# Attention inside a feed-forward kernel: working on whole pairs of heads at a time

## The chip, the cores and the metric

The kernel runs on one core of one Trainium2 chip. A core has five instruction queues that run beside each other and meet through semaphores: TensorE (PE in the profile; its weight loads are listed apart as PEld), VectorE (DVE), ScalarE (ACT), GpSimd (POOL) and SyncE (SP), which here only issues DMAs. Each queue works strictly in the order in which its instructions were written. The metric is the device time of one launch in microseconds (us), as the median of several runs.

## The reference

Two things are computed one after the other. First comes causal attention with a window of 128 positions and a slope per head, for 8 batches of 8 heads, 576 positions and 64 channels:

```
scores = q @ k.T / sqrt(64) + bias(head, distance)      # kept where 0 <= distance < 128
attn   = exp(scores - max) / (sum + 1e-9)
x      = (attn @ v), heads side by side                 # 4608 tokens x 512
```

Then a feed-forward layer with 2048 hidden channels, `out = mish(x @ w_in) @ w_out`, where `mish(h) = h * tanh(log(1 + exp(h)))`. All data is float32.

## The kernel before

**Tiling.** One batch is one chunk of 512 queries; the last 64 queries of every batch are collected in DRAM and form a ninth chunk at the end. Heads go in four pairs, two heads on the upper and lower 64 partitions. A pair's 512 queries are worked in two halves of two blocks of 128 queries each; the pair's last 64 queries are a third, small unit.

**Feed-forward.** Numbers are split in a high and a low part, so that one float32 product is three fast products. `first` multiplies a chunk's `x` with a block of `w_in` (tiles `h`, 192 matmuls of 512 columns a chunk), ACT applies mish and writes `g`. `parts` splits a piece of `g`: ACT writes the high part, POOL subtracts to get the low one (tile `gs`, three buffers). `second` multiplies `gs` with `w_out` into the two PSUM tiles `po` (again 192 matmuls a chunk, in 32 calls of six). `out_tile` and the copies to `ob` bring the result out.

**Attention.** Per unit: `scores` (PE, tiles `s`), `exps` (DVE adds the bias and finds the row's extreme in one instruction, the custom operation `pz<-s,nb`, called the peak here; ACT takes the exponential and its row sum), `fold` (POOL adds the two key blocks so that one transpose serves both; DVE inverts the row sum), `scale` (DVE, `pz<-pz,sm`), `weights` (PE transposes into the `s` tile, DVE multiplies with two triangular masks back into `pz`) and `values` (PE, tile `o`). After the second half `split_hi` (ACT) and `split_lo` (DVE) write the pair's part of `x`. The tiles of the last queries end in `l` (`pz_0l`, `pt_0l`).

**What sets the order.** Attention of batch c+1 is laid between the matmuls of `second` of chunk c. Every step has a number; all steps of a stretch are sorted by it, and every engine gets its instructions in this order. The matmul calls of `second` stand at 0, 1, ..., 31. An attention step at time s (one unit of s is a half of a pair) stands at 30/9·s − 0.2. The step times are written by hand at the ends of `unit` and `last_unit`. Nothing moves afterwards: a queue that waits holds everything behind it.

**Shared buffers.** The `s` tiles (two in PSUM) serve the scores of a half, then its transposes, and `h` in the other stretch. `gs` has three buffers, so `parts` of a piece waits until PE has read the piece three before it. The two weight blocks in `LATE` are only rebuilt from their packed form (sign on ACT, bits on DVE, high on ACT, low on DVE) while chunk 0's `second` runs.

**Lines.** Every instruction of these helpers goes through one recording layer, so the profile gives line L30 for nearly all; the tile names tell them apart.

## Time and profile before

| | |
|---|---|
| median of 3 runs | 1012.8 us (1011.31 to 1013.88) |
| profiled execution, time | 1013.15 us |
| profiled execution, span of the instructions | 1011.4 us |
| granted TensorE clock, mean | 0.995 |
| PE busy | 990.9 us (98%) |
| DVE / ACT / POOL busy | 389.5 / 380.9 / 263.9 us |
| HBM read and written | 50.00 and 10.49 MB, 60 GB/s over the span |

The profile has a page and views that are asked for. In the timeline each row is a run of equal instructions: start, time until the last of them ends, engine, operation, `out<-in` by tile names, shape, count, and in brackets idle time before it with what ended it. Matmuls overlap in the pipeline, so a row's length is more than its share of the engine: how long a piece really occupies PE is read from its start to the start of the next row. PE lists a float32 matmul of 64-row or 64-column tiles as two records. The chain of waits lists which engine's work ended last, piece by piece.

### The profile page before, as it was taken

The page shows a single profiled execution, that of the slowest core. Times are in us where ns is not written, and L with a number is a line of the kernel's source. Part 1 is how long each engine was busy: PE and PEld are TensorE (multiplying, and loading weights), DVE is VectorE, ACT ScalarE, POOL GpSimd, SP SyncE. Part 2 cuts the span into 40 slices and gives each one's busy share as a digit, 9 for nine tenths or more (in the row PEclk, how much of TensorE's full clock was granted, in tenths as well). Part 3 has the DMA queues.
Part 4 walks back from the last instruction along what each step waited for, and adds up shares of the span by engine and source line. Part 5 has one row for each costly group of instructions (what it writes and reads, how often), then busy time and mean ns, then how long its engine had stood idle before and what let it go on. Part 6 is the DMA issues. An engine that isn't in the chain of part 4 may idle for free.

```text
span 1011.4 us, 13792 instructions
## 1 busy us (share of the span) xinstructions
PE 990.9 (98%) x5308; PEld 781.4 (77%) x5308; DVE 389.5 (39%) x1118; ACT 380.9 (38%) x898; POOL 263.9 (26%) x230
## 2 busy tenths in 40 slices
PE   7799899999999999999999999999999999999998
PEld 4588678877787778877787778877887778888886
DVE  5797962047501771066303760067204750000000
ACT  4875542154313442254214432344215431331221
POOL 4310441044202440034203330153104420240043
PEclk8999999999999999999999999999999999999999
DMA  9930221003200231012200221022100200010001
GB/s 369 420 144 1 67 77 61 1 28 101 69 8 0 73 96 36 1 49 81 75 0 27 79 66 34 1 67 79 60 1 28 76 19 27 1 42 21 1 6 37
DMA packets 23393, 61.38 MB, mean 61 GB/s; under 512 B 6688, under 2 KB 7840, under 8 KB 21280
## 3 DMA queue, kind: packets, MB, share of 16 engines
q1 hardware_dynamic: 22096, 59.78, 17.1%
q8 instruction: 42, 0.69, 0.3%
q10 hardware_dynamic: 1232, 0.72, 0.2%
q14 instruction: 23, 0.19, 0.1%
HBM read 50.00 MB, written 10.49 MB: 60 GB/s over the span
## 4 chain that ended last, share of the span: by engine, by line
PE 87%; POOL 0%; DVE 0%; ACT 0%; issue 0%
PE po L30 38%; PE h L30 34%; PE s L30 9%; PE o L30 5%; PE pt_2l L30 0%; PE pt_3l L30 0%; PE pt_1l L30 0%; PE pt_0l L30 0%; POOL pz L30 0%; DVE pz L30 0%; ACT ob L30 0%
## 5 line engine op out<-in xcount | busy, mean ns | idle before, releaser
L30 PE MATMUL po<-so,gs 128*128 128x512 f32 x1728 | 429.1, 398 | 0.0
L30 PE MATMUL h<-x,si 128*128 128x512 f32 x1728 | 393.6, 389 | 1.2 <-DVE si L30 1.2
L30 PEld LDWEIGHTS h<-x,si 128*128 128x128 f32 x1728 | 324.2, 188 | 69.1 <-DVE si L30 1.7
L30 POOL TENSOR_TENSOR gs<-g,gs 128x512 fp32r<-128x512 f32 x144 | 190.0, 1323 | 713.2 <-ACT gs L30 644.4
L30 PEld LDWEIGHTS po<-so,gs 128*128 128x128 f32 x1728 | 314.3, 188 | 72.6 <-ACT x L30 7.0
L30 DVE CUSTOM_DVE_ANT_0 pz<-s,nb 128x256 f32<-128x256 f32 (+1 forms) x256 | 84.5, 386 | 297.1 <-PE s L30 296.4
L30 ACT ACTIVATE pz<-pz,mx 128x256 f32<-128x256 f32 (+1 forms) x256 | 120.4, 471 | 152.0 <-DVE mx L30 150.7
L30 ACT ACTIVATE g<-h 128x1024 f32<-128x1024 f32 x72 | 74.0, 1027 | 272.4 <-PE h L30 272.4
L30 ACT ACTIVATE gs<-g 128x512 fp32r<-128x512 f32 x144 | 88.5, 622 | 45.7 <-PE po L30 45.7
L30 PE MATMUL s<-qk 64*128 64x256 f32 (+1 forms) x624 | 85.3, 369 | 3.8 <-DMA qk<-in_qk_dram 3.8
L30 DVE TENSOR_TENSOR pz<-s,masks 128x1024 f32<-128x1024 f32 x56 | 68.5, 1223 | 24.8 <-PE s L30 24.8
L30 DVE TENSOR_TENSOR pz<-pz,sm 128x512 f32<-128x512 f32 x56 | 53.1, 948 | 56.8 <-POOL pz L30 56.7
L30 PEld LDWEIGHTS s<-qk 64*128 64x128 f32 x624 | 54.7, 192 | 26.1 <-issue 18.9
L30 POOL TENSOR_TENSOR pz<-pz 128x256 f32<-128x256 f32 (+1 forms) x56 | 57.7, 1030 | 0.0
L30 DVE COPY ob<-po 128x512 f32<-128x512 f32 x18 | 12.4, 691 | 117.2 <-PE po L30 117.2
L30 PE MATMUL o<-pz,va 128*64 128x128 f32 (+1 forms) x560 | 54.9, 325 | 0.0
L30 PEld LDWEIGHTS o<-pz,va 128*64 128x64 f32 x560 | 33.3, 136 | 27.8 <-issue 12.3
L30 ACT ACTIVATE x<-o 128x512 fp32r<-128x512 f32 x32 | 19.0, 594 | 85.1 <-PE o L30 85.1
L30 ACT ACTIVATION_READ_ACCUMULATOR pz<-pz,mx 128x1 f32 x256 | 48.0, 187 | 0.0
L30 PE MATMUL s<-ident,pz 128*128 128x128 f32 x280 | 43.4, 283 | 4.4 <-DVE pz L30 1.9
L30 PEld LDWEIGHTS s<-ident,pz 128*128 128x128 f32 x280 | 35.2, 145 | 14.4 <-issue 4.5
L30 DVE TENSOR_SCALAR sm<-sm 128x4 f32<-128x4 f32 x64 | 29.1, 455 | 18.8 <-ACT pz L30 18.8
(120 smaller groups left out, 359.6 us busy)
## 6 DMA issues: line engine op xcount, KB each, us to landing
qk<-in_qk_dram SPq DMA_DIRECT2D x31, 640.0 KB, 4.8
va<-in_v_dram SPq DMA_DIRECT2D x28, 320.0 KB, 2.9
wi<-in_moe_w_in_dram SPq DMA_DIRECT2D x8, 1024.0 KB, 14.3
wo<-in_moe_w_out_dram SPq DMA_DIRECT2D x8, 1024.0 KB, 20.5
out_dram<-ob SPq DMA_DIRECT2D x32, 256.0 KB, 2.0
qk<-in_v_dram SPq DMA_DIRECT2D x4, 320.0 KB, 6.6
xr<-xs SPq DMA_DIRECT2D x4, 256.0 KB, 2.6
out_dram<-ob SPq DMA_DIRECT2D x8, 128.0 KB, 2.3
```

The lines of the kernel that those rows point to most:

```text
L30: ins = method(*args, **kwargs)
```

## The change

Attention of batches 1 to 7 (inside `second` of chunks 0 to 6) is put in another order:

- A step is now placed at 4·s + 0.8 instead of 30/9·s − 0.2, and both halves of a pair and its last queries share one time base, two units of s to a pair. Their scores stand together, all nine transposes stand together, and all value products stand together, followed at once by the scores of the next pair.
- The peaks on DVE are steps of their own (`peak`), ahead of the exponentials of both halves; fold and scale of the second half come a little later than those of the first.
- The value products of the last pair come behind all matmuls of the chunk's `second`. The first `h` tile of the next chunk therefore takes the last pair's part of `x` last, for both of its halves.
- Taking `po` out is its own step (`store`), two steps later for the second half of a chunk, into a buffer of the ring of `g` tiles instead of one of attention's.
- The two late weight blocks get new places in chunk 0: the first is rebuilt ahead of the first pair's peaks, the second around the second pair.
- The load of a later pair's `v` is issued one unit of s earlier. Batch 0 keeps its order.

On PE, first pair of batch 4 inside chunk 3. Before, from the scores of the second half on (`s_0_1` is the second half's score tile, `s_0_0` the first half's, `s_1_0` belongs to the next pair):

```order
L30 MATMUL s_0_1_3410<-qk_0_2881 128x256 x4
L30 MATMUL po_0_0_3364<-so_780,gs_0_2_3361 128x512 x6
L30 MATMUL s_0_0_3347<-ident,pz_0_0_3356 128x128 x4
L30 MATMUL pt_0l<-ident,pz_0l 128x128
L30 MATMUL po_0_1_3375<-so_780,gs_0_2_3361 128x512 x6
L30 MATMUL po_0_0_3364<-so_813,gs_0_3_3387 128x512 x6
L30 MATMUL o_0_3465<-pz_0_0_3356,va_0_3011 64x256 x2
L30 MATMUL o_0_3465<-pz_0_0_3356,va_0_3011 64x128 x2
L30 MATMUL pt_0l<-pf_0l,va_0_3011 64x64 x4
L30 MATMUL s_1_0_3477<-qk_1_3023 128x128 x2
L30 MATMUL s_1_0_3477<-qk_1_3023 128x256 x2
L30 MATMUL s_1_0_3477<-qk_1_3023 128x96 x2
```

And the same place now:

```order
L30 MATMUL s_0_1_3362<-qk_0_2920 128x256 x4
L30 MATMUL s_0_0_3357<-qk_0_2920 128x96 x2
L30 MATMUL po_0_1_3391<-so_742,gs_0_0_3315 128x512 x6
L30 MATMUL po_0_0_3350<-so_748,gs_0_1_3318 128x512 x6
L30 MATMUL po_0_1_3391<-so_748,gs_0_1_3318 128x512 x6
L30 MATMUL po_0_0_3350<-so_780,gs_0_2_3347 128x512 x6
L30 MATMUL po_0_1_3391<-so_780,gs_0_2_3347 128x512 x6
L30 MATMUL po_0_0_3350<-so_813,gs_0_3_3401 128x512 x6
L30 MATMUL s_0_0_3357<-ident,pz_0_0_3371 128x128 x4
L30 MATMUL s_0_1_3362<-ident,pz_0_1_3382 128x128 x4
L30 MATMUL pt_0l<-ident,pz_0l 128x128
L30 MATMUL po_0_1_3391<-so_813,gs_0_3_3401 128x512 x6
```

Between a pair's scores and its transposes there are now six calls of `second`, 36 matmuls, for both halves at once.

On DVE, the same pair now, from behind its peaks (`sm` holds row sums, `pz_0_1` is the second half):

```order
L30 TENSOR_SCALAR sm_0_0_3370<-sm_0_0_3370 128x4
L30 RECIPROCAL sm_0_0_3370<-sm_0_0_3370 128x4
L30 TENSOR_TENSOR pz_0_0_3371<-pz_0_0_3371,sm_0_0_3370 128x4x128
L30 TENSOR_SCALAR sm_0l<-sm_0l 128x1
L30 RECIPROCAL sm_0l<-sm_0l 128x1
L30 TENSOR_TENSOR pz_0l<-pz_0l 128x64
L30 TENSOR_SCALAR pz_0l<-pz_0l,sm_0l 128x128
L30 TENSOR_SCALAR sm_0_1_3381<-sm_0_1_3381 128x4
L30 RECIPROCAL sm_0_1_3381<-sm_0_1_3381 128x4
L30 TENSOR_TENSOR pz_0_1_3382<-pz_0_1_3382,sm_0_1_3381 128x4x128
L30 TENSOR_TENSOR pz_0_0_3371<-s_0_0_3357,masks 128x2x4x128
L30 TENSOR_TENSOR pz_0_1_3382<-s_0_1_3362,masks 128x2x4x128
```

Before, the masks of the first half stood ahead of the second half's sums and scale; now the second half's scale is the last piece of work ahead of both masks, with the last queries' four instructions in front of it.

On POOL, the same pair now (`pz_0_0` and `pz_0_1` are the folds of the two halves, `gs` the low parts of `parts`):

```order
L30 TENSOR_TENSOR gs_0_2_3347<-g_1_3207,gs_0_2_3347 128x512
L30 TENSOR_TENSOR pz_0_0_3371<-pz_0_0_3371 128x2x128
L30 TENSOR_TENSOR gs_0_3_3401<-g_1_3207,gs_0_3_3401 128x512
L30 TENSOR_TENSOR pz_0_1_3382<-pz_0_1_3382 128x4x128
L30 TENSOR_TENSOR gs_0_4_3430<-g_2_3260,gs_0_4_3430 128x512
L30 TENSOR_TENSOR gs_0_5_3447<-g_2_3260,gs_0_5_3447 128x512
```

POOL's order of kinds is nearly the one of before (fold, low part, fold, low part); what moved is when the folds come due.

The diff, cut to its core:

```diff
-        def exps(a):
+        def peak(a):
             ...
+            mx, pz = st["mx"], st["pz"]
+            n = 256 if blocks[a] else P
+            for c in (a, a + 2):
+                dve.tensor_tensor_reduce(
+                    out=pz[:, c, :n], in0=st["s"][c // 2][:, 256 * (a + 1) - n : 256 * (a + 1)],
+                    in1=nb[:, p, c // 2, 256 - n :], scale=-SCALE, scalar=3.0e38,
+                    op0=ALU.add, op1=ALU.min, accum_out=mx[:, c : c + 1],
+                )
+
+        def exps(a):
             mx, sm, pz = st["mx"], st["sm"], st["pz"]
             ...
         return [
-            (0, scores), (0.02, lambda: exps(0)), (0.25, lambda: exps(1)), (0.7, fold), (0.95, scale),
-            (1.3, weights), (1.99, values), (2.02, split_hi), (2.02, split_lo),
+            (0, scores), (0.02 + t, lambda: peak(0)), (0.025 + t, lambda: peak(1)),
+            (0.026 + 27 * t, lambda: exps(0)), (0.026 + 27 * t, lambda: exps(1)), (0.27 + 33 * t, fold),
+            (0.33 + 33 * t, scale), (1.53, weights), (1.99, values), (2.02, split_hi), (2.02, split_lo),
         ]
             ...
-            (0.01, scores), (0.5, exps), (0.9, fold), (1.4, weights), (1.995, values),
+            (0.01, scores), (0.04, peak), (0.31, exps), (0.5, fold), (1.54, weights), (1.995, values),
             ...
-        for k in range(2 * NP):
-            p, half = divmod(k, 2)
-            for u in [unit(b, p, half)] + ([last_unit(b, p)] if half == 0 else []):
-                steps += [(k + d, f) for d, f in u]
+        for p in range(NP):
+            units = [(2 * p, unit(b, p, 0)), (2 * p, last_unit(b, p)), (2 * p + (b == 0), unit(b, p, 1))]
+            steps += [(k + d, f) for k, u in units for d, f in u]
             ...
+        split = NCC - 1 if c and j == 0 else NCC
+        for t, cc in [(t, cc) for r in (range(split), range(split, NCC)) for t in range(2) for cc in r]:
             ...
-            if half or c + 1 >= B:
+            if half:
+                obs[c, half] = big_g(f"ob{c}_{half}")[:, : 2 * DM].rearrange("p (t n) -> p t n", t=2)
+            elif c + 1 >= B:
             ...
+                if m % NJ == NJ - 1:
+                    late = 2 if m == n // 2 - 1 and c + 1 < B else 0
+                    steps.append((2 * m + t + late, lambda m=m, t=t: store(c, m // NJ, t)))
             ...
-        for k, w in enumerate(LATE if c == 0 else []):
-            steps.append((k + 2.5, lambda w=w: sign_w(*w)))
-            steps.append((4 * k + 4.5, lambda w=w: bits_w(*w)))
-            steps.append((4 * k + 6.0, lambda w=w: high_w(*w)))
-            steps.append((4 * k + 8.5, lambda w=w: low_w(*w)))
+        for w, times in zip(LATE, ((-0.2, 0.2, 0.4, 0.7), (2.3, 8.4, 8.5, 8.9)) if c == 0 else ()):
+            for f, t in zip((sign_w, bits_w, high_w, low_w), times):
+                steps.append((t, lambda f=f, w=w: f(*w)))
         if c + 1 < B:
-            steps += [((n - 2) / 9.0 * s - 0.2, f) for s, f in attention(c + 1)]
+            steps += [(4 * s + 0.8, f) for s, f in attention(c + 1)]
```

(`t` is 0 for the first half of a pair and 0.01 for the second.)

## The prediction

> **What bounds the kernel now.** First the page's busy times, then the chain of waits in order of time:

> ```profile
> PE 990.9 (98%) x5308; PEld 781.4 (77%) x5308; DVE 389.5 (39%) x1118; ACT 380.9 (38%) x898; POOL 263.9 (26%) x230
> ...
> 498.75 43.52 PE h L30 x192
> ...
> 609.99 43.52 PE h L30 x192
> ```

> PE is never idle for long and the chain is PE alone. A chunk repeats every 609.99 − 498.75 = 111.24 us. Two stretches of 192 plain matmuls take 2 × 43.52 (0.2267 each), so the attention laid between them costs PE 24.2 us a chunk. Only these 24.2 us, and the few stalls of chunk 0, can change. The timeline of PE for one pair (first pair of batch 5):

> ```profile
> 543.52 5.72 PE L30 MATMUL po<-so,gs 128*128 128x512 f32 x24
> 549.17 1.13 PE L30 MATMUL s<-qk 64*128 64x256 f32 x8
> 550.24 1.66 PE L30 MATMUL po<-so,gs 128*128 128x512 f32 x6
> 551.73 0.60 PE L30 MATMUL s<-ident,pz 128*128 128x128 f32 x4
> ...
> 552.20 3.00 PE L30 MATMUL po<-so,gs 128*128 128x512 f32 x12
> 555.13 0.87 PE L30 MATMUL o<-pz,va 128*64 128x256 f32 x8
> ...
> 556.16 1.54 PE L30 MATMUL s<-qk 64*128 64x128 f32 x12
> 557.48 1.63 PE L30 MATMUL po<-so,gs 128*128 128x512 f32 x6
> 558.95 0.60 PE L30 MATMUL s<-ident,pz 128*128 128x128 f32 x4
> 559.31 3.00 PE L30 MATMUL po<-so,gs 128*128 128x512 f32 x12
> 562.23 1.09 PE L30 MATMUL o<-pz,va 128*64 128x128 f32 x12
> 563.25 1.14 PE L30 MATMUL s<-qk 64*128 64x256 f32 x8
> 564.32 1.66 PE L30 MATMUL po<-so,gs 128*128 128x512 f32 x6
> ```

> No idle time in brackets: DVE, ACT and POOL finish in time for every transpose. What a group costs PE is read from the first `po` row before it to the first `po` row after it, less 0.2267 per matmul.

> **What the change takes from PE.** By that rule four transposes cost 1.83 − 1.36 = 0.47 (557.48 to 559.31), five cost 0.60 (550.24 to 552.20), eight score records alone 1.28 (543.52 to 550.24), twelve value records with eight score records 2.29 (559.31 to 564.32). The same records inside a group cost less, as narrow windows of the timeline show, each cut to start inside the eight score records:

> ```profile
> 563.79 0.60 PE L30 MATMUL s<-qk 64*128 64x256 f32 x4
> 564.00 0.38 PE L30 MATMUL s<-qk 64*128 64x256 f32 x2
> ```

> Two records run side by side in 0.215 us, but from the last two (564.00) to `po` (564.32) it takes 0.32, as it does from 563.25 on at the other end. So eight more score records in a group already open cost 4 × 0.215 = 0.86, and twelve value records (eight half as wide) 4 × 0.11 + 2 × 0.215 = 0.87. Now per chunk:

> - Three times values and scores of a half join the other half's: 2.29 − 0.86 − 0.87 = 0.56 each, 1.7.
> - The first scores, eight records joined: 1.28 − 0.86 = 0.42. The last values, twelve records joined: alone they cost between 2.29 − 1.28 = 1.01 and, like the scores, 1.28; less 0.87 that is 0.14 to 0.41, and I take 0.35.
> - Nine transposes cost 0.60 + 4 × 0.11 = 1.04 against 0.47 + 0.60: 0.03 each, 0.15 with the last queries' transpose that twice stood alone.

> Sum 2.6 to 2.7 us a chunk; I take 2.7, 18.9 for seven. Matmuls and weight loads are the same in number.

> **What it asks of the other queues.** Before, each half had its own 8 us from scores to transposes (543.52 to 551.73). Now both halves and the last queries share one gap of 36 matmuls: 8.16 and about 0.13 for the slower start after scores, 8.29, and the second half's transposes come 4 × 0.11 later, at 8.73 after the first `po`. Do the queues make that? The rows:

> ```profile
> 557.74 0.29 DVE L30 CUSTOM_DVE_ANT_0 pz<-s,nb 128x128 f32<-128x128 f32 x1 [0.45 <-PE s L30]
> ...
> 562.97 0.68 DVE L30 TENSOR_TENSOR pz<-pz,sm 128x512 f32<-128x512 f32 x1
> ```

> ```profile
> 552.14 0.62 ACT L30 ACTIVATE gs<-g 128x512 fp32r<-128x512 f32 x1
> 552.66 0.49 ACT L30 ACTIVATE pz<-pz,mx 128x256 f32<-128x256 f32 x1
> ...
> 553.93 0.63 ACT L30 ACTIVATE gs<-g 128x512 fp32r<-128x512 f32 x1 [0.19 <-PE po L30]
> 558.15 0.40 ACT L30 ACTIVATE pz<-pz,mx 128x128 f32<-128x128 f32 x1 [3.59 <-DVE mx L30]
> ...
> 558.55 0.39 ACT L30 ACTIVATE pz<-pz,mx 128x128 f32<-128x128 f32 x1
> ...
> 558.94 0.49 ACT L30 ACTIVATE pz<-pz,mx 128x256 f32<-128x256 f32 x1
> ...
> 559.43 0.49 ACT L30 ACTIVATE pz<-pz,mx 128x256 f32<-128x256 f32 x1
> ```

> First peak 0.26 after the first `po` (557.48 to 557.74), first exponential 0.41 later: 0.67. ACT's order is four exponentials (2 × 0.40 + 2 × 0.49), a `gs` (0.52 to the next start), four exponentials (4 × 0.49), the last queries' one (0.49 as bound), the next `gs` (call it A). The second half's exponentials end at 0.67 + 1.78 + 0.52 + 1.96 + 0.1 for the sum's read: 5.0; A ends at 4.9 + 0.5 + 0.62 = 6.0. DVE's peaks are done by then. The second fold starts on POOL at 5.1. Then this, from the same profile:

> ```profile
> 548.07 1.28 POOL L30 TENSOR_TENSOR gs<-g,gs 128x512 fp32r<-128x512 f32 x1 [0.61 <-ACT gs L30]
> ...
> 554.09 1.29 POOL L30 TENSOR_TENSOR pz<-pz 128x512 f32<-128x512 f32 x1
> 555.33 1.27 POOL L30 TENSOR_TENSOR gs<-g,gs 128x512 fp32r<-128x512 f32 x1
> ```

> ```profile
> 548.10 1.34 DVE L30 TENSOR_SCALAR pz_0l<-pz_0l,sm_0l 128x128 f32<-128x128 f32 x1
> ...
> 555.41 1.74 DVE L30 TENSOR_TENSOR pz<-pz,sm 128x512 f32<-128x512 f32 x1 [1.04 <-POOL pz L30]
> ```

> The scale takes 0.68 alone, but 1.74 when a POOL subtraction began 0.08 before it: it ends 0.55 after POOL's does (556.60, 557.15). The last queries' multiply, begun 0.03 behind a subtraction, ends 0.09 after it. Such DVE work stands still until POOL's running instruction is over. Before, that fell into slack.

> [...]

> Now: fold 5.1 to 6.34 (554.09 to 555.33 until POOL goes on), A's subtraction 6.34 to 7.61. The last queries' multiply is behind it: 7.70. Sum and inverse of the second half, 0.2 each:

> ```profile
> L30 DVE RECIPROCAL sm<-sm 128x4 f32<-128x4 f32 x64 | 11.4, 178 | 2.2
> ```

> so the scale issues at 8.1. The subtraction after A, B, waits for the `gs` buffer that PE frees after 30 of the 36 matmuls, 6.93; ACT starts 0.24 after PE's last read (552.20 + 1.49 to 553.93), 7.17, ends 7.80, POOL starts B at 7.88. That is 0.2 ahead of the scale. B ends at 9.15, the scale 0.55 later: 9.70. From a scale's end to a waiting transpose:

> ```profile
> 109.88 1.44 DVE L30 TENSOR_TENSOR pz<-pz,sm 128x512 f32<-128x512 f32 x1
> ...
> 111.46 0.63 PE L30 MATMUL s<-ident,pz 128*128 128x128 f32 x4 [1.21 <-DVE xo_0l L30]
> ```

> 0.14. The second half's transposes start at 9.84 instead of 8.73: a **stall of 1.1 us per pair**, with everything on PE queued behind it. It hits pairs 0 to 2; behind the fourth pair's fold no subtraction is due. The masks follow on DVE while PE runs twelve matmuls, as before, so values should not wait. Per chunk: −2.7 + 3 × 1.1 = +0.6.

> **Chunk 0** is different, since DVE now rebuilds a weight block ahead of the first peaks. Its pieces in the trace:

> ```profile
> 105.48 0.68 DVE L30 TENSOR_SCALAR to<-wo 128x1024 uint32<-128x1024 uint32 x1
> 106.20 2.19 DVE L30 SCALAR_TENSOR_TENSOR to<-wo,to 128x1024 uint32<-128x1024 uint32 x1
> ...
> 113.89 1.22 DVE L30 TENSOR_TENSOR so<-to,so 128x1024 fp32r<-128x1024 f32 x1
> ```

> ```profile
> 108.48 1.06 ACT L30 ACTIVATE so<-to 128x1024 fp32r<-128x1024 f32 x1 [1.16 <-DVE to L30]
> ```

> In a chain they take 5.15, after a sign step that runs while the scores do; nothing covers them, so I take 5.1 for pair 0 (bounds: 2, if only 3 us of it stands behind the scores; 6.2, with the 1.1 on top). Pair 1 gets 1.1 and the second block's 1.2 inside its peaks, pair 2 gets 1.1: 8.5. Before, chunk 0 stalled for 1.21 (quoted) and:

> ```profile
> 120.17 0.64 PE L30 MATMUL s<-ident,pz 128*128 128x128 f32 x4 [1.65 <-DVE pz L30]
> ```

> with 0.3 more in the second pair's other half: 3.2. So +5.3.

> The rest costs nothing that I can find: the first `h` tile asks for the late `x` only after 18 matmuls (4.1 us), behind which an ACT and a DVE step of 0.6 to 0.7 fit; loads and stores have several us.

> **Sum.** −18.9 + 6 × 3.3 + 5.3 = +6.2 on the profiled 1013.15, which is 0.35 above the median: **1019 us**, 0.6% slower. Bounds of the stall, 0.9 to 1.3 a pair (0.2 either way on 9.84), give 1015 to 1023.

> **Rivals.** 1. *The scale gets in first.* My margin is 0.2 in a chain of 8 us. If B starts late or DVE is 0.2 early, the scale ends at 8.8, the stall is 0.2, and chunk 0 adds 3.5: −18.9 + 3.6 + 3.5 = −11.8, **1001**, faster. For it: the narrow margin; against: B hangs on PE's pace, which hardly varies, and the scale on POOL's. The point of decision is 8.73. 2. *It differs by pair.* Two of three pairs blocked: −18.9 + 6 × 2.4 + 4.4 = 0, **1013**. For it: pair 1 has `x` and `ob` work on the same queues. 3. *PE gains only half*, if openings cost the same in longer groups: +1.35 a chunk, **1028**; against it are the quoted 0.215 steps.

> **How the numbers follow.** Forecast 0.56, rival 1 0.22, rival 2 0.16, rival 3 0.06. About 3 us (0.3%) is what a measurement can tell from no change. Slower: the forecast and rival 3, 0.62; same: most of rival 2, 0.14; faster: rival 1 and the rest of 2, 0.24. Range 1000 to 1025; the forecast's own is 1015 to 1023.

> **What would show it.** PE's timeline: one group of values and scores a pair, its cost by the rule above near 4.2 with both halves (before 2.56 + 2.29); idle of about 1.1 in front of the second half's four transposes in pairs 0 to 2 and none in pair 3, released by DVE; a scale of 1.6 us behind a subtraction on POOL. Chunks would repeat every 111.8 us. With transposes that never wait, at 108.5, rival 1 holds; a stall of 1.1 under another releaser would leave my chain wrong though the time be right.

## The result, and the profile after

The changed kernel takes **1023.63 us** (median, 1022.18 to 1024.49) against 1012.05 us for the kernel before: a ratio of 1.0111, 95% interval 1.0091 to 1.0132. It is slower by 1.1%. The profiled execution took 1023.82 us with a span of 1022.1, 10.67 more than the profiled execution of before.

The page's busy times, and under them the two rows of the chain of waits that show a chunk's period (chunks 4 and 5, rows of `h`):

```profile
PE 979.1 (96%) x5308; PEld 790.9 (77%) x5308; DVE 425.3 (42%) x1118; ACT 377.8 (37%) x898; POOL 261.0 (26%) x230
```

```profile
506.48 43.74 PE h L30 x192
...
618.57 43.74 PE h L30 x192
```

PE is busy 11.8 us less (990.9 before), and yet the program is longer: PE now stands still. DVE is busy 36 us more with the same 1118 instructions. A chunk repeats every 112.09 us (112.07 over chunks 1 to 7) instead of 111.23. PE's waits, as total, number and longest:

```profile
PE s L30 <- DVE pz L30: 23.9, 21, 3.1
```

21 waits are three in each of seven chunks, in front of the transposes. This is PE's timeline for the first pair of batch 5, the place that the prediction walked through, with the fourth pair's transposes at the end:

```profile
553.70 8.46 PE L30 MATMUL po<-so,gs 128*128 128x512 f32 x36
561.99 0.60 PE L30 MATMUL s<-ident,pz 128*128 128x128 f32 x4
563.56 0.63 PE L30 MATMUL s<-ident,pz 128*128 128x128 f32 x4 [0.97 <-DVE pz L30]
...
564.06 3.02 PE L30 MATMUL po<-so,gs 128*128 128x512 f32 x12
567.00 1.74 PE L30 MATMUL o<-pz,va 128*64 128x256 f32 x20
...
571.09 8.45 PE L30 MATMUL po<-so,gs 128*128 128x512 f32 x36
...
614.13 1.04 PE L30 MATMUL s<-ident,pz 128*128 128x128 f32 x8
```

There is one group of values and scores a pair. The second half's transposes wait 0.97 in the pair shown, as in the two pairs after it; the fourth pair's eight run through. What DVE and POOL do meanwhile:

```profile
560.14 1.21 DVE L30 TENSOR_SCALAR pz_0l<-pz_0l,sm_0l 128x128 f32<-128x128 f32 x1
...
561.74 1.68 DVE L30 TENSOR_TENSOR pz<-pz,sm 128x512 f32<-128x512 f32 x1
```

```profile
558.73 1.29 POOL L30 TENSOR_TENSOR pz<-pz 128x512 f32<-128x512 f32 x1 [0.50 <-ACT pz L30]
559.98 1.29 POOL L30 TENSOR_TENSOR gs<-g,gs 128x512 fp32r<-128x512 f32 x1
561.60 1.27 POOL L30 TENSOR_TENSOR gs<-g,gs 128x512 fp32r<-128x512 f32 x1 [0.33 <-ACT gs L30]
```

The three POOL rows are the fold and subtractions A and B. The last queries' multiply lasts 1.21 and ends 0.08 behind A (the fourth pair's, at 612.27 and with no subtraction beside it, lasts 0.28); B then starts 0.14 ahead of the second half's scale, which lasts 1.68 instead of 0.68 and holds PE.

Chunk 0 is the other place. The first three pairs on PE's timeline, and then the view of busy time by windows (start and end, length, busy time of PE, PEld, DVE, ACT and POOL with counts, granted clock, DMA share, GB/s), whose third column from the right is the clock:

```profile
105.12 1.20 PE L30 MATMUL po<-so,gs 128*128 128x512 f32 x4 [1.07 <-ACT gs L30]
106.71 0.74 PE L30 MATMUL po<-so,gs 128*128 128x512 f32 x2 [0.40 <-POOL gs L30]
...
111.06 1.09 PE L30 MATMUL s<-ident,pz 128*128 128x128 f32 x4 [3.14 <-DVE pz L30]
...
112.01 3.88 PE L30 MATMUL po<-so,gs 128*128 128x512 f32 x12
115.82 1.74 PE L30 MATMUL o<-pz,va 128*64 128x256 f32 x20
...
131.19 1.09 PE L30 MATMUL s<-ident,pz 128*128 128x128 f32 x4 [2.38 <-DVE pz L30]
...
136.12 1.74 PE L30 MATMUL o<-pz,va 128*64 128x256 f32 x20
...
150.07 0.63 PE L30 MATMUL s<-ident,pz 128*128 128x128 f32 x4 [0.97 <-DVE pz L30]
...
153.49 0.76 PE L30 MATMUL o<-pz,va 128*64 128x256 f32 x6
```

```profile
110.56:113.86 3.30, 2.80 (x9) 2.45 (x10) 3.16 (x5) 0.00 (x0) 1.48 (x1) 0.50 0.00 0
...
131.09:134.39 3.30, 3.21 (x10) 2.78 (x11) 3.14 (x4) 0.00 (x0) 0.00 (x0) 0.50 0.21 79
```

The waits add up to 7.96 us. In the first pair DVE rebuilds the weight block from 97.03 to 102.29, so the peaks start 5 us late, and with them ACT's exponentials and the `gs` that stands behind four of them. Around the ends of the two longest waits the clock is halved for 3.4 us each time (in the kernel before it stays at 1.00 throughout this chunk). From the waiting transposes to the values PE then takes 4.76 (111.06 to 115.82) and 4.93 (131.19 to 136.12), against 3.42 in the third pair (150.07 to 153.49), so 1.34 and 1.51 more.

### The profile page after: what moved, and what is told of

The parts are those of the page before. It is cut to its first block, busy times and chain, and to the rows that moved or that the text cites. A ratio compares the mean times of both kernels' runs of the same rounds, so it can differ in the third digit from the quotient of the medians.

```text
span 1022.1 us, 13726 instructions
## 1 busy us (share of the span) xinstructions
PE 979.1 (96%) x5308; PEld 790.9 (77%) x5308; DVE 425.3 (42%) x1118; ACT 377.8 (37%) x898; POOL 261.0 (26%) x230
## 4 chain that ended last, share of the span: by engine, by line
PE 76%; DVE 12%; ACT 9%; issue 2%; DMA 0%; POOL 0%; DVEq 0%; POOLq 0%; ACTq 0%
PE h L30 38%; PE po L30 22%; PE s L30 9%; ACT pz L30 7%; PE o L30 5%; DVE pz L30 5%; DVE pz_1l L30 1%; DVE pz_2l L30 1%; DVE pz_0l L30 1%; ACT gs L30 1%; DVE sm L30 1%; PE pt_0l L30 0%; PE pt_1l L30 0%; DVE pf L30 0%; PE pt_3l L30 0%
## 5 line engine op out<-in xcount | busy, mean ns | idle before, releaser
L30 PE MATMUL po<-so,gs 128*128 128x512 f32 x1728 | 411.8, 394 | 1.5 <-ACT gs L30 1.1
L30 PE MATMUL h<-x,si 128*128 128x512 f32 x1728 | 394.5, 390 | 1.2 <-DVE si L30 1.2
L30 PEld LDWEIGHTS h<-x,si 128*128 128x128 f32 x1728 | 323.7, 188 | 69.2 <-DVE si L30 1.7
L30 PEld LDWEIGHTS po<-so,gs 128*128 128x128 f32 x1728 | 321.7, 189 | 67.8 <-ACT gs L30 1.5
L30 POOL TENSOR_TENSOR gs<-g,gs 128x512 fp32r<-128x512 f32 x144 | 186.6, 1300 | 568.4 <-ACT gs L30 545.5
L30 DVE CUSTOM_DVE_ANT_0 pz<-s,nb 128x256 f32<-128x256 f32 (+1 forms) x256 | 82.6, 386 | 310.7 <-PE s L30 310.0
L30 ACT ACTIVATE g<-h 128x1024 f32<-128x1024 f32 x72 | 74.0, 1028 | 273.1 <-PE h L30 273.1
L30 ACT ACTIVATE pz<-pz,mx 128x256 f32<-128x256 f32 (+1 forms) x256 | 119.9, 470 | 70.4 <-DVE mx L30 70.4
L30 ACT ACTIVATE gs<-g 128x512 fp32r<-128x512 f32 x144 | 88.7, 624 | 127.1 <-PE po L30 127.1
L30 POOL TENSOR_TENSOR pz<-pz 128x256 f32<-128x256 f32 (+1 forms) x56 | 57.4, 1024 | 158.1 <-ACT pz L30 158.1
L30 PE MATMUL s<-qk 64*128 64x256 f32 (+2 forms) x624 | 77.8, 360 | 3.8 <-DMA qk<-in_qk_dram 3.8
L30 DVE TENSOR_TENSOR pz<-pz,sm 128x512 f32<-128x512 f32 x56 | 78.9, 1409 | 5.8
L30 PEld LDWEIGHTS s<-qk 64*128 64x128 f32 (+1 forms) x624 | 57.1, 192 | 21.2 <-issue 12.8
L30 DVE TENSOR_TENSOR pz<-s,masks 128x1024 f32<-128x1024 f32 x56 | 65.7, 1212 | 8.0 <-PE s L30 7.9
L30 PE MATMUL s<-ident,pz 128*128 128x128 f32 x280 | 43.6, 289 | 25.1 <-DVE pz L30 23.9
L30 PEld LDWEIGHTS s<-ident,pz 128*128 128x128 f32 x280 | 33.9, 148 | 34.9 <-issue 29.2
L30 DVE COPY ob<-po 128x512 f32<-128x512 f32 x18 | 12.3, 682 | 114.3 <-PE po L30 114.3
L30 ACT ACTIVATE x<-o 128x512 fp32r<-128x512 f32 x32 | 19.0, 594 | 95.0 <-PE o L30 95.0
L30 PE MATMUL o<-pz,va 128*64 128x128 f32 (+1 forms) x560 | 48.7, 320 | 0.0
L30 ACT ACTIVATION_READ_ACCUMULATOR pz<-pz,mx 128x1 f32 x256 | 48.0, 187 | 0.0
L30 PEld LDWEIGHTS o<-pz,va 128*64 128x64 f32 x560 | 33.9, 136 | 18.0 <-issue 7.4
L30 ACT ACTIVATE ob<-po 128x512 f32<-128x512 f32 x18 | 10.7, 596 | 51.4 <-PE po L30 51.4
```

The lines of the kernel that those rows point to most:

```text
L30: ins = method(*args, **kwargs)
```

## The experiments

All are edits of the changed kernel. Times are medians; the ratio is to the kernel before, run beside them, with its 95% interval. Because PE's start differs by over 2 us from run to run (the first `h` matmul stands at 45.75 to 48.09), pieces of profiles are compared from the first `h` on.

### A wait added on POOL

```diff
+        def hold():
+            if half and p + 1 < NP:
+                pool.tensor_tensor(
+                    out=held[:, p : p + 1], in0=st["pz"][:, 3, :1], in1=st["pz"][:, 3, 1:2], op=ALU.add
+                )
...
-            (0.33 + 33 * t, scale), (1.53, weights), (1.99, values), (2.02, split_hi), (2.02, split_lo),
+            (0.33 + 33 * t, scale), (1.53, weights), (1.99, values), (2.02, split_hi), (2.02, split_lo), (1.0, hold),
```

> One tiny POOL instruction is added per pair (pairs 0 to 2 of batches 1 to 7) between subtractions A and B; it reads one column of the second half's scaled tile, so B cannot start before the scale is done. Nothing is taken away. Theory 1 (the running subtraction B holds the scale up): the scale issues at 8.04 behind the pair's first po matmul as now, lasts 0.7 instead of 1.68, and the second half's transposes wait 0.1 to 0.2 instead of 0.97. That is about 0.9 less in each of 18 pairs of chunks 1 to 6, 16.2, and 2 to 3.4 in chunk 0 (the second pair's wait falls from 2.38 to about 1.3, the third's to 0.2; 1.4 of it only if the halved clock behind the 2.38 goes with it): 1023.6 - 18.2 to 19.6 = 1004 to 1005.5, and chunks repeat every 109.3 to 109.5 instead of 112.1. Theory 2 (the transposes wait for DVE's own queue, which has the last queries' work in front of the scale): the added wait helps nothing, the wait of 0.97 stays, 1023 to 1025. Theory 3 (B is needed soon): the transposes no longer wait but matmuls of po do, for POOL's gs; about 1015 to 1023.

Measured: **1001.57 us** (1000.95 to 1003.64), ratio 0.9892 (0.9875 to 0.9908). One more instruction with one more wait on POOL took 22 us off the changed kernel. The timeline of the same pair of batch 5 with this kernel, on PE, DVE and POOL:

```profile
540.77 8.46 PE L30 MATMUL po<-so,gs 128*128 128x512 f32 x36
549.06 1.22 PE L30 MATMUL s<-ident,pz 128*128 128x128 f32 x8
```

```profile
548.81 0.69 DVE L30 TENSOR_TENSOR pz<-pz,sm 128x512 f32<-128x512 f32 x1
```

```profile
549.58 0.19 POOL L30 TENSOR_TENSOR held<-pz 128x1 f32<-128x1 f32 x1 [1.25 <-DVE pz L30]
549.73 1.29 POOL L30 TENSOR_TENSOR gs<-g,gs 128x512 fp32r<-128x512 f32 x1
```

The scale issues at the same 8.04 behind the first `po`, lasts 0.69, and the eight transposes run in one row, 0.18 longer than without any wait (1.22 against 1.04 in the fourth pair above). Subtraction B comes 1.1 us later, and no `po` waits for it. Chunks repeat every 109.13. Theory 1 holds: B alone holds the scale up; theories 2 and 3 fall. The time is 2.4 to 4 us below what I had expected: six periods are 0.2 to 0.4 shorter, and the profiled execution began 2 us earlier than that of the changed kernel.

### The last queries' fold behind the scale

```diff
-            (0.01, scores), (0.04, peak), (0.31, exps), (0.5, fold), (1.54, weights), (1.995, values),
+            (0.01, scores), (0.04, peak), (0.31, exps), (0.67, fold), (1.54, weights), (1.995, values),
```

> The last queries' fold (four DVE instructions, about 0.4 us without the wait of their multiply) goes behind the second half's scale; nothing else. Theory 1 (whoever issues first, scale or B, makes the other wait): the scale now issues near 7.7 behind the first po, ahead of B at 7.9, and lasts 0.7; the wait in front of the second half's transposes is gone, but now the last queries' multiply issues behind B's start and ends with B at about 9.2 to 9.3, so that their one transpose (due at about 9.2 + 0.1) waits about 0.7. Per pair 1.13 lost becomes 0.7 to 0.75: 18 x 0.4 = 7 less and 0.5 to 1 in chunk 0, 1015 to 1016.5. Theory 2 (DVE's own queue is what is late, no matter what POOL does): scale 0.4 earlier but still 1.6 long, wait in front of the transposes 0.97 - 0.4 = 0.55, the last queries' work after it inside the time of the four transposes: 18 x 0.4 = 7 less as well, so the time alone does not tell the two apart: the length of the scale (0.7 or 1.6) and which transpose waits do.

Measured: 1012.57 us (1010.22 to 1014.16), ratio 0.9997 (0.9983 to 1.0010): the changed kernel's loss is gone, nothing is gained. The timeline of the first pair of batch 5 with this kernel, on DVE, POOL and PE:

```profile
552.08 1.76 DVE L30 TENSOR_TENSOR pz<-pz,sm 128x512 f32<-128x512 f32 x1 [0.99 <-POOL pz L30]
...
554.02 1.04 DVE L30 TENSOR_TENSOR pz_0l<-pz_0l 128x64 f32<-128x64 f32 x1
```

```profile
550.75 1.29 POOL L30 TENSOR_TENSOR pz<-pz 128x512 f32<-128x512 f32 x1 [0.51 <-ACT pz L30]
552.00 1.28 POOL L30 TENSOR_TENSOR gs<-g,gs 128x512 fp32r<-128x512 f32 x1
553.63 1.35 POOL L30 TENSOR_TENSOR gs<-g,gs 128x512 fp32r<-128x512 f32 x1 [0.34 <-ACT gs L30]
```

```profile
555.53 0.30 PE L30 MATMUL pt_0l<-ident,pz_0l 128*128 128x128 f32 x1 [0.47 <-DVE pz_0l L30]
```

The median is 2.4 us below the range of theory 1; in the profiled execution (1011.38) the first `h` starts 2.3 earlier than in that of the changed kernel. What theory 1 says of a scale that comes first can be seen in the profile of before: one at 578.05, 0.34 ahead of a subtraction, lasts 0.68, and that subtraction 1.48, where the one at 575.17 lasts 1.30. Theory 1's place of waiting is right (the last queries' transpose, 0.47 instead of the expected 0.7, behind an addition that B makes 1.04 long), but not its working: the scale is not 0.7 long. I had overlooked subtraction A. It follows the fold directly, and the scale, which waits for that fold, finds A 0.08 us old and takes 1.76. It ends in time all the same. Both pieces that DVE started behind a running subtraction lasted until it was over (0.56 and 0.08 us past its end); the edit only moved which subtraction holds what.

### Transposes in two pieces

```diff
-            (0.33 + 33 * t, scale), (1.53, weights), ...
+            (0.33 + 33 * t, scale), (1.53 + 25 * t, weights), ...
-            ... (0.5, fold), (1.54, weights), (1.995, values),
+            ... (0.5, fold), (1.785, weights), (1.995, values),
```

> The second half's and the last queries' transposes come one call of six matmuls later than the first half's (after 42 instead of 36). Theory 1: the scale still lasts 1.6 and ends at 9.7, but the transposes are due at 8.3 + 0.5 + 1.36 = 10.1 and do not wait; pairs 0 to 2 lose no 1.13. Opening PE's transpose group twice costs 0.1 to 0.2 in each of four pairs, and in the fourth pair, where nothing stood still before, the second half's masks come 1.4 later and the values may wait up to 0.7. Per chunk -3.4 + 0.6 + 0.7 = -2.1 to -2.7, six chunks -12.6 to -16; chunk 0 another -2.9, and 1.4 to 2.9 more if its two long waits, now 1.8 and 1.35 by the same count, no longer end at a halved clock: 1002 to 1007. Theory 2 (the scale of the second half is held by something that keeps step with PE, such as the gs buffer): the wait moves along with the transposes and the time stays within 3 us of 1023.6.

Measured: 1001.53 us (998.34 to 1002.09), ratio 0.9881 (0.9862 to 0.9901), 0.5 below the range of theory 1. The scale is still held by B (1.68 us), but six matmuls stand between it and its transposes, and those do not wait. The price stands at the end of a chunk, as expected (0.41 where up to 0.7 was allowed for), here on PE's timeline in batch 5's fourth pair:

```profile
600.38 1.09 PE L30 MATMUL o<-pz,va 128*64 128x128 f32 x12 [0.41 <-DVE pz L30]
```

The period is 109.33. In chunk 0 the longest wait is 1.75, and the granted clock stays at 1.00 behind it.

### The late weight blocks at the places of before

```diff
-        for w, times in zip(LATE, ((-0.2, 0.2, 0.4, 0.7), (2.3, 8.4, 8.5, 8.9)) if c == 0 else ()):
+        for w, times in zip(LATE, ((2.5, 4.5, 6.0, 8.5), (3.5, 8.5, 10.0, 12.5)) if c == 0 else ()):
```

> The two late weight blocks go back to the places of before inside chunk 0; only chunk 0 can change. Theory 1 (chunk 0 loses its stalls plus about 1.45 us of halved clock behind each wait over 2 us): the waits of the first pair go (3.14 and the 1.47 ahead of it), but the second block's bits and the first block's low part now stand directly in front of the second pair's peaks: one wait of 4 to 5 us there. Idle time falls from about 8 to 7, and one stretch at half clock instead of two: -1 - 1.45, about 1021 (1020.5 to 1022). Theory 2 (my prediction's sum: the 5.1 of the first pair and the 1.2 in the second are the price of the new places, the clock plays no part): with the old places chunk 0 stalls 3.2 + 1.1 instead of 8.5, -4.2: 1019.4.

Measured: 1019.47 us (1017.94 to 1020.27), ratio 1.0063 (1.0048 to 1.0079). The time is the one of theory 2, the trace is the one of theory 1: a single long wait in the second pair, on PE's timeline

```profile
126.08 1.46 PE L30 MATMUL po<-so,gs 128*128 128x512 f32 x4 [4.30 <-DVE so L30]
```

with 0.43, 0.37, 0.26 and 0.97 beside it, 6.33 in all, where theory 2 had 4.3. From the first `h` to chunk 1's `h` it is 119.03 against 122.14 in the changed kernel, 3.1 less: 1.6 of it less waiting, the other 1.5 one stretch at half clock instead of two. So chunk 0's excess is not mended by the old places either, since in the new order they stand in front of the second pair's peaks.

### Chunk 0 mended

The edit of the wait on POOL, and:

```diff
         if w in LATE:
+            steps.append((X0 + 30 + n / 4, lambda w=w: sign_w(*w)))
             continue
...
-        for w, times in zip(LATE, ((-0.2, 0.2, 0.4, 0.7), (2.3, 8.4, 8.5, 8.9)) if c == 0 else ()):
-            for f, t in zip((sign_w, bits_w, high_w, low_w), times):
+        for w, times in zip(LATE, ((-0.2, -0.1, 0.0), (8.4, 8.5, 8.75)) if c == 0 else ()):
+            for f, t in zip((bits_w, high_w, low_w), times):
```

> e1_hold, and in chunk 0 the two sign steps of the late weight blocks move into the stretch before (batch 0's feed-forward), the first block's bits, high and low part stand directly ahead of the first po matmul, and the second block's at 8.4 to 8.75. Theory 1 (chunk 0 lost idle time and, behind its long idle time, halved clock): against e1_hold the waits of 1.07 and 0.40 for gs go (no sign and table load ahead of ACT's gs), the first pair's 3.14 falls to 1.0 to 1.5, the second pair's 1.30 to 0.5 to 1.0; no wait reaches 2 us, so the clock stays 1.00 and the matmuls that ran at 0.50 for about 5 us behind the wait of 3.14 save another 2 to 2.9: 1001.6 - (1.5 + 1.8 + 0.6) - 2.5 = 995 (994 to 997). Theory 2 (the halved clock belongs to this place in the program, not to the idle time): only the waits go, 997.5 to 998. Later chunks stay as in e1_hold, 109.1 us apart.

Measured: 997.40 us (996.06 to 998.68), ratio 0.9854 (0.9835 to 0.9873). From the first `h` to chunk 1's it takes 113.54 against 120.00 with the wait on POOL alone: 6.5 less, of which the waits give 3.0 (2.86 against 5.90), and the rest, about 3.4, is clock: there 6.8 us ran at half clock, here none. The row of the view by windows, for the kernel with the wait on POOL alone:

```profile
108.21:114.81 6.60, 5.80 (x17) 4.77 (x17) 5.17 (x6) 1.69 (x2) 2.65 (x4) 0.50 0.00 0
```

The profiled executions differ by only 4.65 (the medians by 4.2), since in the one profiled here the first `h` starts 1.9 later. By its time the run lies between the two theories, 0.4 above the range of theory 1 and 0.1 below that of theory 2; the trace decides, since the clock is 1.00 in the whole chunk and theory 2 wants it halved here. The first pair's wait came out at 2.36 instead of 1.0 to 1.5, because ACT's table load of 1.28 us now stands between the first peak and the first exponential, on ACT's timeline:

```profile
98.50 1.28 ACT L30 ACT_TABLE_LOAD   x1 [1.04 <-DVE mx L30]
```

A wait of 2.36 without half clock behind it, where 2.38 in the changed kernel had it, speaks against a limit on the wait's length. The measurement of the clock below settles this.

### Both edits of the last queries

The edit before, with the fold at 0.67 and `hold` reading the last queries' scaled tile:

```diff
+                    out=held[:, p : p + 1], in0=st["pz"][:, :1], in1=st["pz"][:, 1:2], op=ALU.add
...
-            (0.01, scores), (0.04, peak), (0.31, exps), (0.5, fold), (1.54, weights), (1.995, values),
+            (0.01, scores), (0.04, peak), (0.31, exps), (0.67, fold), (1.54, weights), (1.995, values), (1.0, hold),
```

> e5_best with the last queries' fold behind the second half's scale as in e2_lastfold, and with the tiny POOL instruction reading the last queries' scaled tile instead of the scale's. [...] Theory 2 (the last queries' work is late by itself when it comes last): their transpose waits 0.3 to 0.5 in each of 18 to 21 pairs, 5 to 9 us more than e5_best, 1000 to 1004.

Measured: **993.72 us** (991.42 to 994.06), ratio 0.9819 (0.9799 to 0.9839), the fastest here: 18 to 19 us below the kernel before, 30 below the changed one and 3.7 below the run with chunk 0 mended. Theory 2 falls: nothing waits in pairs 0 to 2 of chunks 1 to 6, and what the wait on POOL had left, (109.13 − 108.61) / 3 = 0.17 per pair, is gone too. The first pair of batch 5 on PE's timeline, and two rows of the chain of waits:

```profile
532.14 8.46 PE L30 MATMUL po<-so,gs 128*128 128x512 f32 x36
540.43 1.04 PE L30 MATMUL s<-ident,pz 128*128 128x128 f32 x8
...
541.34 3.01 PE L30 MATMUL po<-so,gs 128*128 128x512 f32 x12
```

```profile
376.32 43.74 PE h L30 x192
484.92 43.74 PE h L30 x192
```

The period is 108.61. This is the change's own gain with its stall taken away: 111.23 − 108.61 = 2.62 us a chunk.

### The order of the first `h` tile undone

```diff
-        split = NCC - 1 if c and j == 0 else NCC
+        split = NCC
```

> One part of the change undone: the first h tile of chunks 1 to 8 takes its matmuls in the old order again, so that it asks for the last pair's x after 9 matmuls instead of 18. Theory 1 (this part costs and brings nothing): x is complete 1.2 us after the first h matmul (618.50 to 619.70 in chunk 4), it is asked for after 9 x 0.2267 = 2.04; no wait, 1023.6 within 1.5. Theory 2 (it is needed, since values now end directly ahead of h): 0.2 to 0.7 of waiting in each of 7 chunks, 1025 to 1028.5.

Measured: 1023.27 us (1020.89 to 1025.12), ratio 1.0109 (1.0084 to 1.0134); the period is 112.07, as in the changed kernel. This part costs and brings nothing.

### Graded waits

The edit of chunk 0 mended, and in batches 4 to 7, ahead of `hold`:

```diff
+            if half and p + 1 < NP and b >= 4:
+                for _ in range((2, 5, 8, 3, 6, 1, 7, 4, 9, 10, 0, 12)[3 * (b - 4) + p]):
+                    dve.tensor_scalar(
+                        out=st["pz"][:, :, :P], in0=st["pz"][:, :, :P], scalar1=1.0, scalar2=None, op0=ALU.mult
+                    )
```

> A measurement of the clock by itself. To e5_best are added, in pairs 0 to 2 of batches 4 to 7, multiplications by 1.0 of the second half's scaled tile on DVE, behind its scale: 2, 5, 8; 3, 6, 1; 7, 4, 9; 10, 0, 12 of them, about 0.3 to 0.45 us each. The transposes must wait for them, so PE idles for graded lengths, between full work of 9 us and more on either side. Theory 1 (a single idle time decides, between 1.76 us, which left the clock at 1.00 in e3_two, and 2.38 us, which halved it in the changed kernel): waits up to 1.8 cost themselves alone, those over 2.4 are followed by granted clock 0.50 for 2 to 5 us and 1.4 to 2.9 us more. Theory 2 (what counts is idle time summed over some microseconds, since in e2_lastfold 1.39 and 1.88 that lay 1 us apart led to 0.50): for idle times that stand alone the limit is the same in all places and lies between 1.76 and 3.1. Theory 3 (the halving belongs to chunk 0): the clock stays 1.00 behind waits of 3 and 4 us here. By theory 1, about 995 + 67 x 0.4 + 5 x 2 = 1030.

Measured: 1038.98 us (one execution); each multiplication takes 0.46. Waits of 0.46, 0.90, 1.36, 1.83 and 2.29 left the clock at 1.00; those of 2.75, 3.23, 3.67, 4.13, 4.60 and 5.52 were followed by 0.50, in the middle of the program, so theory 3 falls. Three of them on PE's timeline, and the view by windows behind them:

```profile
455.41 0.63 PE L30 MATMUL s<-ident,pz 128*128 128x128 f32 x4 [2.29 <-DVE pz L30]
...
475.48 1.08 PE L30 MATMUL s<-ident,pz 128*128 128x128 f32 x4 [3.67 <-DVE pz L30]
```

```profile
671.90 0.63 PE L30 MATMUL s<-ident,pz 128*128 128x128 f32 x4 [3.23 <-DVE pz L30]
```

```profile
455.41:458.41 3.00, 3.00 (x16) 2.58 (x17) 3.00 (x4) 0.83 (x2) 1.36 (x2) 1.00 0.23 87
475.38:478.68 3.30, 3.20 (x10) 2.78 (x11) 2.64 (x3) 0.00 (x0) 1.41 (x2) 0.50 0.00 0
...
671.90:673.20 1.30, 1.30 (x9) 1.16 (x10) 1.30 (x2) 0.00 (x0) 1.30 (x2) 1.00 0.00 0
673.30:676.60 3.30, 3.30 (x10) 2.44 (x8) 1.05 (x2) 0.63 (x1) 1.22 (x1) 0.50 0.00 0
676.70:679.00 2.30, 2.30 (x32) 1.73 (x32) 0.07 (x1) 0.30 (x1) 0.00 (x0) 1.00 0.03 7
```

Behind the wait of 3.23 PE works 1.3 us at full clock before the clock falls. In these rows a fall does not follow from the wait's own end or length, and half clock lasts 3.4 us (475.29 to 478.70, for one), or 6.8 behind the waits of 4.13 and 5.52 (710.81 to 717.64 and 833.69 to 840.52 in windows of 0.1 us). The last section draws this together. The time is 9 us above my estimate: 2.4 because its base, the kernel with chunk 0 mended, took 997.4 instead of 995, 4 for 67 multiplications of 0.46 instead of 0.40, and the rest is half clock: eight times 3.4 us behind six waits, where five waits had been counted at 2 us each.

## Why the prediction was right, and where it was not

1019.0 was predicted and 1023.6 measured: slower, as forecast, by the mechanism forecast, but by 10.7 us in the profiled execution instead of 6.2. The measured time lies inside the stated range of 1000 to 1025, and 0.6 above the 1015 to 1023 that the prediction gave for its own mechanism. Step by step:

- **What PE gains.** Predicted 2.7 us a chunk, 2.62 measured without waits. Nine transposes come to 1.04 as predicted (541.34 − 532.14 − 36 × 0.2267), a pair's values and scores to 4.31 by the rule used there (571.09 − 564.06 − 12 × 0.2267), against "near 4.2". Rival 3, half the gain, falls.
- **The stall.** Behind the first `po` at 553.70 the fold starts at 5.03 (predicted 5.1), A at 6.28 (6.34), B at 7.90 (7.88), the scale at 8.04 (8.1), it ends at 9.72 (9.70), and the transposes start at 9.86 (9.84). They are 1.13 late, of which the profile books 0.97 as idle; the whole cost of a pair's wait is (112.07 − 108.61) / 3 = 1.15. It stands in pairs 0 to 2 and not in pair 3, with DVE's `pz` as releaser, as predicted. That the subtraction is the cause was an inference from durations; the added wait on POOL, which leaves DVE's order as it is, shows it. Rival 2, a stall that differs by pair, falls: the three are alike to 0.01.
- **Later chunks.** Predicted +0.6 each, measured +0.84 (0.08 from the gain, 0.05 from each of three stalls): 1.4 us over six chunks.
- **Chunk 0, the step that failed.** The prediction put its cost at +5.3 for waits and −2.7 for the gain. The waits add up nearly as predicted: 4.61 in the first pair (1.07, 0.40, 3.14) for 5.1, 2.38 for 2.3, 0.97 for 1.1, together 7.96 against 3.16 before, so +4.8. Their place is partly another: 1.47 of the first pair's stands in front of `po`, which waits for `gs`. What the sum lacked is what follows them: it priced a wait at its length, though around the ends of the two long ones the clock is halved for 3.4 us each, and the work behind them takes 1.34 + 1.51 = **2.85 us** more. Before, the longest wait in this chunk was 1.65 and nothing of the kind followed.
- **The total.** 6.2 − 0.5 (the waits of chunk 0, +4.8 for +5.3) + 2.85 + 1.4 = 10.0, against 10.67. Of the missing 0.7, about 0.3 stands in chunk 0 (5.28 more than before from its first `h` to chunk 1's, where these terms give 4.95) and 0.3 behind chunk 7's first `h`; what they are is open.
- **The rest at nothing.** Undoing the order of the first `h` tile changed nothing (1023.27). The other parts (the stores' new buffer, the earlier load) were not tried by themselves; no wait in the profile names them.
- **Rival 1.** Its condition, the scale ahead of B, was not met by 0.14 us. That such a scale would keep its length stood on no row of the prediction, but the profile of before shows it (0.68 at 578.05). The wait on POOL enforces the condition, and gives 1001.57 where the rival had 1001. The period is the rival's (109.13 against 111.24 − 2.7 + 0.6); that the whole time agrees so well is partly luck: chunk 0 costs 2.3 more than the rival had, and the first `h` of that profiled execution starts 1.95 earlier than in the kernel before.

So the change's idea is sound: with one ordering constraint, the last queries' fold moved behind the scale and the late blocks moved, the same grouping gives 993.7.

## What to carry to other kernels

When work is gathered into longer groups, the engine that gains is paid at once, while the others get one common deadline in place of several: walk their chain to the tenth of a microsecond, and look for work of one engine that lengthens another's, as POOL's subtraction did with DVE's scale (1.68 us beside it, 0.69 without). If an unimportant instruction on one engine gets ahead of an important one on another, an added dependency that orders the two can be the cheapest repair. And a long wait on PE can cost more than its length, in the changed kernel 1.34 and 1.51 us more: in the runs here every wait of 2.38 us or more inside the chunks was followed by half clock, none of 1.75 or less that stood alone was, and in between it depended on where the wait lay (2.29 and 2.36 were not).

## What the runs showed of the hardware that was not expected

**In these traces PE's clock changed on a fixed grid.** In windows of 0.1 us, the mean clock in the run with graded waits is between 0.50 and 1.00 in those in which it returns:

```profile
478.68:478.78 0.10, 0.10 (x2) 0.07 (x1) 0.00 (x0) 0.00 (x0) 0.00 (x0) 0.89 0.00 0
577.68:577.78 0.10, 0.10 (x2) 0.10 (x1) 0.00 (x0) 0.10 (x1) 0.00 (x0) 0.95 0.00 0
676.60:676.70 0.10, 0.10 (x2) 0.00 (x0) 0.00 (x0) 0.00 (x0) 0.06 (x1) 0.62 0.00 0
799.53:799.63 0.10, 0.10 (x2) 0.10 (x1) 0.00 (x0) 0.10 (x1) 0.00 (x0) 0.87 0.00 0
```

By these sums a wait of 2.38 halved the clock (2.19 of it fell into one stretch), waits of 2.29 and 2.36 did not (1.69 and 0.60; 1.29 and 1.07), and in the run with the last queries' fold behind the scale two waits of 1.39 and 1.88, 0.6 us apart, together did (1.81 in one stretch). Which waits cost another 1.5 us or more is thus chance, as far as a kernel's author can tell, between 1.8 and 3.4 us; these bounds are an estimate from the 1.81 and from two stretches of 1.72 side by side. A wait of up to 1.75 us that stood alone never did from the first `h` on.

Ahead of the first `h`, in the attention of batch 0, idle time alone does not decide. In the kernel before, the stretch from 8.03 to 11.45 has 1.69 us idle and was followed by half clock, and the next, up to 14.86, has none and did not bring the full clock back; the changed kernel shows the same pair (1.69 from 8.12 to 11.53, then none up to 14.95). Later there, the stretch from 38.75 to 42.16 in the kernel before, with 2.15 us idle, was followed by one stretch at half clock. What else counts there is open.

**In the profile the lengthened scale starts on time.** In batch 5's first pair it issues 8.04 behind the first `po` both when it lasts 1.68 and when, with the wait on POOL, it lasts 0.69. Of the 36 us by which DVE is busier with the same instructions, 26 are the scale's: its mean over 56 went from 948 to 1409 ns. The row of the groups after:

```profile
L30 DVE TENSOR_TENSOR pz<-pz,sm 128x512 f32<-128x512 f32 x56 | 78.9, 1409 | 5.8
```

So a duration that doubled here with the shape unchanged (0.69 to 1.68) was a wait that no row of waits names.
